# More of a fused retention and two-layer kernel's second layer by two levels of Strassen

## The chip, the cores and the metric

One core of a Trainium2 chip runs the kernel. The time is device microseconds, median of three runs. One further execution was taken by the hardware profiler; its lines are what the text reads. Engines: PE is TensorE (PEld its weight loads), DVE is VectorE, ACT ScalarE, POOL GpSimd, SP SyncE, which issues most DMAs.

## The reference

```python
# attention: B, H, S, D = 4, 8, 768, 64, one state per head with decay gamma
for t in range(S):
    state = gamma[None, :, None, None] * state + np.einsum('bhd,bhe->bhde', k[:, :, t], v[:, :, t])
    y[:, :, t] = scale * np.einsum('bhd,bhde->bhe', q[:, :, t], state)
# two layers on 3072 tokens of 512: w_in is 512 x 2048, w_out is 2048 x 512
h = x @ w_in
g = np.maximum(0.01 * h, h)
return (g @ w_out).astype(np.float32)
```

All matrix products are float32.

## The kernel before

**Chunks and units.** The sequence of 768 is cut into NC = 6 chunks of C = 128 tokens; with 4 batches a chunk is 512 tokens. The 2048 hidden columns are cut into NU = 4 units of 512. Chunks 0 and 1 are done first, together. For chunks 2 to 5 a loop over `n` from 0 to 15 runs unit `u = n % 4` of chunk `c = 2 + n // 4`; "unit 7" in this document is `n = 7`. Each unit has a first-layer part and a second-layer part, and the loop is skewed: in iteration n the second layer of unit n and the first layer of unit n + 1 are done.

**Strassen.** A 512 x 512 product of blocks of 256 is done as seven products M1 to M7 instead of eight; blocks are summed first (S and T blocks) and the seven results are summed after. In a *one-level* product each of the seven is four matmuls of 128x128 weights and 256 columns. In a *two-level* product it is again split by Strassen into seven of 128x128 weights and 128 columns. The first layer is two-level: `inner(n, 0)` does four of its seven products side by side ("group 0", 4 x 7 matmuls), `inner(n, 1)` the other three ("group 1"). Before, second-layer units 4 to 14 do M1, M5, M6 and M7 one-level (`trunk`) and M2, M3 and M4 two-level (`leaf_steps`); units 0 to 3 and 15 do all seven one-level (`output`). The profile records each float32 matmul twice, so a one-level product is 8 records and a two-level product 14.

**One iteration.** The order is written by hand, and every engine runs its own instructions in that order. In units 4 to 14: VectorE's `differences` for unit n's second layer (four), group 0 of unit n + 1 and its three VectorE sums, `outer(n + 1, 0)` (two VectorE sums); in units 0, 1, 4, 5, 8 and 9 (`visiting`) the visit of the attention for two batches of the next chunk (`joint_visit`); in `u == 1`, `differences` of the next chunk's x; in `u == 2` and `u == 3` the sums of its blocks (`sums_of_x`). Then `leaf_sums` on GpSimd (four differences, 384 columns each), three steps of the trunk, in units 0, 1, 4, 5 and 8 `scores_of_pair` for the next two batches, the rest of the trunk's sums into `o`, group 1 of unit n + 1 with three VectorE sums, `outer(n + 1, 1)` (five VectorE sums; four leaky activations on ScalarE), and the leaf: 7 x 3 matmuls.

**Banks.** Groups 0 and 1 accumulate in PSUM banks 0 to 3; in each, ScalarE copies M1's result from bank 0 into bank 3, on which M6 accumulates. M5 and M3 use bank 1, M4 bank 2. The trunk uses banks 5 (A: M1), 4 (B) and 7 (C: M5). The leaf uses 6, 7, 2 and 5. The visit uses 0, 7, 1 and 2, the scores 0 to 3. A bank is used again when its readers are done.

**The output tile.** `o` collects a chunk's result over four units; all chunks from the second on share one buffer, so the first write of a chunk (in unit 4, 8 or 12, a ScalarE copy) waits until the stores of the chunk before have left it. Leaf results go into `o` by a DMA of GpSimd that adds to its destination (`accum_op`, line 1283), except at the end of a chunk (units 7 and 11), where VectorE adds them and SyncE stores (1287, 1288).

**The attention in the loop.** `joint_visit(c, b)` ends by loading v of the pair that follows (`of_pair`, line 138, on SyncE; the buffer is free when the visit's matmuls are done) and scaling it on GpSimd (`decay_v`, 163, two instructions). `scores_of_pair` of the same iteration reads it on TensorE (382), one half for each instruction; its products of q and k come just before (371).

**Second-layer weights of the leaf.** The row sums of the weights (`sums_of_rows`, VectorE, in units 0 to 3) are written to DRAM (`leaf_kept`), and loaded before each leaf by `load_rows` (1235, SyncE): at the end of the unit before, or in the middle of a visiting unit. First-layer weights stream in as `wa` (group 0) and `wb` (group 1) by `load_unit`, also on SyncE.

**The last unit.** Unit 15 is one-level, in the order M1, M5, M6, M4, M2, M7, M3; M5 and M3 end in three pieces. Its M5 reads the first of `differences(15)`.

Of the kernel before, what the change touches and what calls it, by code (L numbers as in the profile page):

```python
# [18 lines left out]
C = 128  # L19
# [3 lines left out]
def kernel(  # L23
# [587 lines left out]
    def plus(out, a, b):  # L611
        nc.vector.tensor_tensor(out=out, in0=a, in1=b, op=ALU.add)  # L612
# [195 lines left out]
    last_three = {}  # L808
# [9 lines left out]
    def new_g(c, u):  # L818
        i = slot[0]
        slot[0] = 1 - i  # L820
        both = work.tile([128, 7, 2, N], FP32, tag=f"g{i}", name=f"g_{c}_{u}")
        last_three[c, u] = both[:, 2:5]
        return u, both[:, 0:4], Reversed(both)
# [360 lines left out]
    leaf_kept = [dram.tile([128, 3, 7, C], FP32, name=f"leaf_kept_{u}") for u in range(NU)]  # L1184
# [3 lines left out]

    def leaf_rooms():

        free = [flat_of(unit(k)[:, 2:5]) for k in (1, 3, 5)]
        spare = [x2_place[0][:, 21 * C :], streamed_flat[0][:, 21 * C :]]
        more = [spare[i // 2][:, ds(i % 2 * 3 * C, 3 * C)] for i in range(4)]
        return free, spare, [x.rearrange("p (q n) -> p q n", q=3) for x in more]

    def rows_of(u):

        if u < NU - 1:
            return [((0, 3, 1), unit(2 * u + 1)[:, 2:5])]
        return [((0, 3, 2), units[2 * u + 1][1]), ((1, 2, 1), last_s4)]  # L1200

    def sums_of_rows(u):

        free, _, more = leaf_rooms()
        if u == NU - 1:
            more = more[0:2] + [x[:, 7 * C : 10 * C].rearrange("p (q n) -> p q n", q=3)
                                for x in free[0:2]]
        bases = []
        for at, blocks in rows_of(u):
            which = slice(*at)  # L1210
            a11, a21, a12, a22 = (blocks[:, :, k, ts(m, C)] for k in range(2) for m in range(2))
            r = [x[:, which] for x in more]
            plus(r[0], a21, a22)
            minus(r[1], r[0], a11)
            minus(r[2], a12, r[1])
            minus(r[3], a11, a21)
            bases.append((which, blocks))

        def keep():
            for which, blocks in bases:  # L1220
# [4 lines left out]
            for j, r in enumerate(more):  # L1225
                nc.sync.dma_start(out=leaf_kept[u][:, :, 3 + j], in_=r)
        return keep

    def load_rows(n):

        free, spare, _ = leaf_rooms()
        leaf_weights[:] = [x[:, 0 : 7 * C].rearrange("p (j n) -> p j n", j=7)
                           for x in (free[0], free[1], spare[1])]
        for to, kept_rows in zip(leaf_weights, (leaf_kept[at_of(n)[1]][:, i] for i in range(3))):
            nc.sync.dma_start(out=to, in_=kept_rows)
# [3 lines left out]
    def by_leaves(n):  # L1239
        return n >= NU and n < N2 - 1  # L1240

    def leaf_sums(n):

        free, spare, _ = leaf_rooms()
        made = [x.rearrange("p (q n) -> p q n", q=3)
                for x in (free[0][:, 7 * C : 10 * C], free[1][:, 7 * C : 10 * C],
                          spare[0][:, 0 : 3 * C])]
        three = last_three[at_of(n)]
        b11, b12, b21, b22 = (three[:, :, k, ts(h, C)] for k in range(2) for h in range(2))
        for out, a, b in ((made[0], b12, b11), (made[1], b22, made[0]), (made[2], b21, made[1]),  # L1250
                          (b12, b22, b12)):
            nc.gpsimd.tensor_tensor(out=out, in0=a, in1=b, op=ALU.subtract)
        return [b11, b21, *made, b22, b12]

    def leaf_steps(n, moving):

        ps = [bank[i][:, 0 : 3 * C].rearrange("p (i n) -> p i n", i=3) for i in (6, 7, 2, 5)]
        results = leaf_results()
        for m, q, j, s in INNER:
            for i in range(3):  # L1260
                nc.tensor.matmul(ps[q][:, i], lhsT=leaf_weights[i][:, j], rhs=moving[s][:, i],  # L1261
# [14 lines left out]
    def leaf_results():  # L1276
        return flat_of(unit(5)[:, 2:5]).rearrange("p (i q n) -> p i q n", i=3, q=4)

    def leaf_results_taken(c, o, final):

        results = leaf_results()
        if not final:
            nc.gpsimd.dma_start(out=o[:, 0:3].rearrange("p i k n -> p (i k n)"),  # L1283
                                in_=results.rearrange("p i q n -> p (i q n)"), accum_op=ALU.add)
            return
        for i in range(3):
            plus(o[:, i], o[:, i], results[:, i].rearrange("p (k h) n -> p k (h n)", k=2))
            nc.sync.dma_start(out=out[c, i], in_=o[:, i])

    def trunk(c, o, part, first, final):  # L1290

        u, g, gd = part
        ps = {x: room[x] for x in "ABC"}
        for m, x, sa, rhs, start in (("M1", "A", 0, g[:, 0], True), ("M5", "C", 4, gd[:, 0], True),
                                     ("M6", "B", 5, gd[:, 1], False),
                                     ("M7", "B", 1, g[:, 1], False)):
# [7 lines left out]
            elif m == "M6":  # L1304
                if first:
                    nc.scalar.copy(out=o[:, 1], in_=ps["B"])
                else:
                    plus(o[:, 1], o[:, 1], ps["B"])
            elif m == "M7":
                yield  # L1310
                if first:
                    nc.scalar.copy(out=o[:, 2], in_=ps["B"])
                    plus(o[:, 3], o[:, 3], ps["B"])
                else:
                    plus(o[:, 2:4], o[:, 2:4],
                         ps["B"].unsqueeze(1).to_broadcast([128, 2, 2, N]))
                if final:
                    nc.sync.dma_start(out=out[c, 3], in_=o[:, 3])
            yield

    def trunk_taken(o, first):

        if first:
            nc.scalar.copy(out=o[:, 0], in_=room["A"])
            nc.scalar.copy(out=o[:, 3], in_=room["C"])
            plus(o[:, 1], o[:, 1], room["C"])
        else:
            plus(o[:, 0], o[:, 0], room["A"])
            plus(o[:, 1:4:2], o[:, 1:4:2],
                 room["C"].unsqueeze(1).to_broadcast([128, 2, 2, N]))  # L1330
# [43 lines left out]
    def outer(n, group, later=None):  # L1374
# [17 lines left out]
        if group == 0:  # L1392
            plus(u2, u2, m1)
            plus(to(1), u2, m5)
            return
# [47 lines left out]

    held = []
    for n in range(N2):
# [4 lines left out]
        visiting = c + 1 < NC and u < 2  # L1450
# [4 lines left out]
        if n + 1 < N2:  # L1455
# [6 lines left out]
            outer(n + 1, 0)  # L1462
        if visiting and u == 0:
            xs[c + 1] = new_x(c + 1)
        if visiting:
# [7 lines left out]
        moving = leaf_sums(n) if by_leaves(n) else None  # L1473
        scores_next = visiting and following(c + 1, 2 * u)
        part = gs.pop(n)
        if by_leaves(n):
            steps = trunk(c, os[c], part, u == 0, u == NU - 1)
# [3 lines left out]
        products(steps, 3)  # L1481
        if scores_next:
            scores_of_pair(*scores_next)
        if visiting:
            load_unit(n + 2, 0)
        if by_leaves(n):
            if scores_next and u > 0:
                products(steps, 2)
            trunk_taken(os[c], u == 0)
            if scores_next and u == 0:  # L1490
                products(steps, 2)
        else:
            products(steps, 1)
        if c == 2:
            keep = sums_of_rows(u)
        if more:
# [3 lines left out]
            if c == 2:  # L1500
                keep()
            products(steps, 1)
            later = [] if by_leaves(n) else None
            outer(n + 1, 1, later)
        if by_leaves(n):
            products(steps, 1)
# [104 lines left out]
```

## Time and profile before

| | us |
|---|---|
| median of 3 runs | 633.54 (633.47 to 634.14) |
| profiled execution | 633.81 |
| its span | 632.1 |
| TensorE busy | 624.7 |
| VectorE busy | 498.1 |
| ScalarE busy | 283.5 |
| GpSimd busy | 81.4 |

Units 0 to 15 take the span from about 251 us on. Unit 7 starts at 427.79, unit 8 at 450.33, unit 9 at 477.32, unit 12 at 548.1 and unit 15 at 616.1. A table of busy time by stretch (start:end, length, busy TensorE, weight loads, VectorE, ScalarE and GpSimd with counts, granted clock, DMA share, GB/s), of units 6, 7, 8, 9 and 12:

```profile
405.20:427.80 22.60, 22.60 (x175) 21.77 (x174) 18.93 (x33) 10.60 (x23) 5.17 (x5) 1.00 0.98 306
427.80:450.30 22.50, 22.50 (x174) 21.67 (x174) 20.55 (x28) 10.06 (x21) 5.84 (x5) 1.00 0.81 240
450.30:477.30 27.00, 27.00 (x399) 25.64 (x398) 18.24 (x33) 11.86 (x24) 6.15 (x8) 1.00 0.64 218
477.30:503.00 25.70, 25.00 (x303) 23.64 (x302) 21.35 (x33) 10.51 (x23) 5.65 (x7) 1.00 0.77 224
548.10:571.00 22.90, 22.82 (x175) 21.81 (x174) 15.91 (x26) 12.02 (x26) 5.15 (x4) 1.00 0.77 247
```

The clock column is 1.00 in all of them. In a timeline a line such as `x4` is a run of neighbouring instructions; what stands in brackets is the idle time before it and what ended it. A DMA's line on SPq or POOL is its issue; it lands later.

### The profile page before, as it was taken

Reading aid. Unit: us, or ns where it says so; the run is one execution under the profiler, and the core shown is the slowest. Engines: PE = TensorE matmul, PEld = TensorE weight load, DVE = VectorE, ACT = ScalarE, POOL = GpSimd, SP = SyncE. Lnnn points to the kernel's source line nnn. Section 1 sums busy time; section 2 is a strip of 40 time slices with the busy share of each in tenths; the row PEclk is TensorE's granted clock in tenths of the full one; section 3 lists DMA queues with packets and bytes.
Section 4 is the critical chain, followed back from the end, with each engine's and each line's share of the span. In section 5 each row is a group of like instructions: output and inputs, shape, how many; then the busy total and the mean of one; then the engine's idle time right before and its main releaser. Section 6 shows DMA issues by size and latency. Waiting matters only on the chain.

```text
span 632.1 us, 15063 instructions
## 1 busy us (share of the span) xinstructions
PE 624.7 (99%) x6284; PEld 570.5 (90%) x6284; DVE 498.1 (79%) x803; ACT 283.5 (45%) x559; POOL 81.4 (13%) x98
## 2 busy tenths in 40 slices
PE   8999999999999999999999999999999999999997
PEld 5888888888888889899999999999998999999996
DVE  5679769889979976668887768799848889866765
ACT  5876646347443114352442452634434424544540
POOL 2000000000011010101000033313033023033200
PEclk9999999999999999999999999999999999999999
DMA  8941325547772998295964888998479579689724
GB/s 330 404 138 34 133 67 208 163 145 226 260 276 81 334 350 289 89 347 168 340 209 157 280 293 250 342 293 260 157 240 306 159 230 278 206 263 271 192 45 116
DMA packets 103219, 141.18 MB, mean 223 GB/s; under 512 B 4328, under 2 KB 82024, under 8 KB 103152
## 3 DMA queue, kind: packets, MB, share of 16 engines
q1 hardware_dynamic: 101552, 132.53, 63.3%
q0 software_dynamic: 1296, 7.08, 5.6%
q8 instruction: 49, 0.80, 0.5%
q10 hardware_dynamic: 304, 0.62, 0.3%
q14 instruction: 18, 0.15, 0.1%
HBM read 108.49 MB, written 24.64 MB: 211 GB/s over the span
## 4 chain that ended last, share of the span: by engine, by line
PE 90%; DMA 5%; ACT 2%; DVE 2%; issue 0%; SPq 0%; DVEq 0%; ACTq 0%
PE bank L1348 26%; PE bank L1299 12%; PE bank L668 11%; PE bank L1261 8%; PE C_h L668 4%; PE B_o L668 4%; PE A_h L668 4%; PE A_o L668 4%; PE C_o L668 4%; PE B_h L668 4%; PE D_o L668 2%; PE D_h L668 2%; DMA x_words<-in_weights_dram 1%; DMA wa<-kept 1%; DMA in<-in_kv_dram 1%; PE bank L371 1%
## 5 line engine op out<-in xcount | busy, mean ns | idle before, releaser
L612 DVE TENSOR_TENSOR made<-made,bank 128x512 f32<-128x512 f32 (+1 forms) x96 | 56.1, 617 | 39.9 <-PE bank L1348 35.9
L1348 PEld LDWEIGHTS bank<-x,wb 128*128 128x128 f32 x672 | 77.6, 192 | 1.1 <-ACT bank L1352 0.3
L1348 PE MATMUL bank<-x,wb 128*128 128x128 f32 x672 | 77.9, 275 | 0.1
L612 DVE TENSOR_TENSOR o<-o,bank 128x512 f32<-128x512 f32 (+3 forms) x75 | 55.2, 767 | 24.3 <-ACT bank L782 6.2
L615 DVE TENSOR_TENSOR g<-g 128x512 f32<-128x512 f32 x96 | 64.1, 688 | 5.3 <-ACT g L1390 0.6
L1348 PE MATMUL bank<-x,wa 128*128 128x128 f32 x512 | 67.6, 275 | 0.0
L1299 PE MATMUL bank<-g,w 128*128 128x256 f32 x288 | 66.1, 382 | 0.7 <-DVE x L468 0.7
L1348 PEld LDWEIGHTS bank<-x,wa 128*128 128x128 f32 x512 | 62.8, 192 | 0.3
L1299 PEld LDWEIGHTS bank<-g,w 128*128 128x128 f32 x288 | 53.2, 190 | 8.0 <-DVE x L468 1.1
L1348 PE MATMUL bank<-t,wa 128*128 128x128 f32 x384 | 53.4, 275 | 0.1
L1348 PEld LDWEIGHTS bank<-t,wa 128*128 128x128 f32 x384 | 48.0, 192 | 0.3 <-DMA wa<-kept 0.3
L612 DVE TENSOR_TENSOR g<-made 128x512 f32<-128x512 f32 x64 | 44.0, 709 | 3.0
L1352 ACT COPY bank<-bank 128x512 f32<-128x512 f32 (+1 forms) x32 | 16.6, 520 | 60.1 <-PE bank L1348 59.8
L1390 ACT ACTIVATE g<-g 128x512 f32<-128x512 f32 x64 | 38.5, 631 | 8.2 <-DVE g L612 8.2
L668 PE MATMUL bank<-g,w 128*128 128x256 f32 x168 | 38.0, 382 | 0.0
L668 PEld LDWEIGHTS bank<-g,w 128*128 128x128 f32 x168 | 31.3, 190 | 4.2
L668 PE MATMUL bank<-g,last 128*128 128x256 f32 (+1 forms) x148 | 32.6, 375 | 0.0
L668 PEld LDWEIGHTS bank<-g,last 128*128 128x128 f32 x148 | 27.0, 190 | 3.9 <-DVE g L615 0.4
L1261 PE MATMUL bank<-g,w 128*128 128x128 f32 x176 | 26.8, 275 | 0.0
L668 PE MATMUL A_h<-x,w 128*128 128x256 f32 x112 | 26.6, 380 | 0.0
L1303 ACT COPY bank<-bank 128x512 f32<-128x512 f32 x11 | 6.3, 570 | 41.1 <-PE bank L1299 41.1
L1283 POOL DMA_DIRECT2D o<-w x9 | 8.1, 903 | 125.2 <-DVE g L615 65.6
(255 smaller groups left out, 1234.8 us busy)
## 6 DMA issues: line engine op xcount, KB each, us to landing
wa<-kept SPq DMA_DIRECT2D x16, 1344.0 KB, 9.4
raw<-in_weights_dram SPq DMA_DIRECT2D x31, 512.0 KB, 4.4
wb<-kept SPq DMA_DIRECT2D x16, 896.0 KB, 5.5
w<-leaf_kept SPq DMA_DIRECT2D x22, 448.0 KB, 4.6
wa<-kept SPq DMA_DIRECT2D x16, 448.0 KB, 6.1
wb<-kept SPq DMA_DIRECT2D x16, 448.0 KB, 6.3
o<-w POOLq DMA_DIRECT2D x9, 768.0 KB, 9.2
out_dram<-o SPq DMA_DIRECT2D x23, 256.0 KB, 2.5
```

The lines of the kernel that those rows point to most:

```text
L371: nc.tensor.matmul(at[j][ts(h, 64), n, m, i], lhsT=x[ts(j, 64), 1, a, ts(h, 64)], rhs=x[ts(j, 64), 0, a, ts(h, 64)], start=(n == 0 and a = ...
L612: nc.vector.tensor_tensor(out=out, in0=a, in1=b, op=ALU.add)
L615: nc.vector.tensor_tensor(out=out, in0=a, in1=b, op=ALU.subtract)
L668: nc.tensor.matmul(to, lhsT=block(w, sa)[:, k, ts(i, 128)], rhs=rhs[:, k, a:z], start=(first and (i == 0 or split) and n == 0 and k == 0), ...
L1261: nc.tensor.matmul(ps[q][:, i], lhsT=leaf_weights[i][:, j], rhs=moving[s][:, i], start=(i == 0 and m in ("M1", "M5", "M4")), stop=True, sk ...
L1283: nc.gpsimd.dma_start(out=o[:, 0:3].rearrange("p i k n -> p (i k n)"), in_=results.rearrange("p i q n -> p (i q n)"), accum_op=ALU.add)
L1299: nc.tensor.matmul(ps[x][:, i, :], lhsT=block(2 * u + 1, sa)[:, k, ts(i, 128)], rhs=rhs[:, k, :], start=(start and i == 0 and k == 0), sto ...
L1303: nc.scalar.copy(out=ps["B"], in_=ps["A"])
L1348: nc.tensor.matmul(ps[q][:, i], lhsT=w[:, j, i], rhs=part_of(moving[i], s), start=(i == 0 and m in ("M1", "M5", "M4")), stop=True, skip_gr ...
L1352: nc.scalar.copy(out=ps[3], in_=ps[0])
L1390: nc.scalar.activation(g[:, i], g[:, i], AF.Prelu, alpha=0.01)
```

## The change

Units 2 to 14 are now done by leaves (`ON_CHIP`, `by_leaves`), and M7 joins M2, M3 and M4 in the leaf, which is 7 x 4 matmuls over 512 columns; the trunk keeps M1, M5 and M6. All four results go through `results` (512 columns wide), whose third block gets the fourth added by VectorE, and always by the accumulating DMA into all of `o`; at the end of a chunk, now also in unit 3, four stores on SyncE follow that DMA. The sums of the trunk go into `o` after its third step: in the first unit of a chunk by two ScalarE copies (512 and 1536 wide) and one VectorE sum, else by VectorE sums of 512, 1024 and 1536. The scores come after two trunk products instead of three.

Rows of M7 are summed and kept as well (four blocks; the sets for units 0 and 1 of a chunk with block M7 apart, in room left by the tile `u2`). The sets for u = 2 and 3 stay in one place in unit 1's weight tile for the leaves of units 2 and 3; set 1 and set 2 are both made in unit 1, set 3 on GpSimd in unit 3 (12 instructions). In unit 9 the first of GpSimd's differences waits for the last VectorE sum of `outer(n + 1, 0)`.

```diff
-        last_three[c, u] = both[:, 2:5]
+        last_four[c, u] = both[:, 1:5]
...
+    ON_CHIP = range(2, NU)
+    def by_leaves(n):
+        return ON_CHIP[0] <= n < N2 - 1
...
-    def sums_of_rows(u):
+    def sums_of_rows(u, engine=nc.vector):
...
+        if u in ON_CHIP:
+            flat = free[1].rearrange("p (r q n) -> p r q n", r=4, q=4)
+            parts = [(slice(0, 4), [flat[:, r] for r in range(4)])]
+        else:
+            (_, blocks), = rows
+            rows = [(slice(0, 1), blocks[:, 0:1]), (slice(1, 4), blocks[:, 1:4])]
...
+            for n, a, b in ((0, a21, a22), (1, r[0], a11), (2, a12, r[1]), (3, a11, a21)):
+                engine.tensor_tensor(out=r[n], in0=a, in1=b, op=ALU.subtract if n else ALU.add)
...
+            for which, r in parts:
+                for j in range(4):
+                    nc.sync.dma_start(out=leaf_kept[u][:, which, 3 + j], in_=r[j])
...
-    def leaf_sums(n):
+    def leaf_sums(n, behind=None):
...
-            nc.gpsimd.tensor_tensor(out=out, in0=a, in1=b, op=ALU.subtract)
+            op = nc.gpsimd.tensor_tensor(out=out, in0=a, in1=b, op=ALU.subtract)
+            if behind is not None:
+                tc.add_manual_dep(op.ins, behind.ins.name, IN_ORDER, reason="one port for both")
+                behind = None
...
+    TARGETS = (3, 0, 1, 2)
...
-            for i in range(3):
-                nc.tensor.matmul(ps[q][:, i], lhsT=leaf_weights[i][:, j], rhs=moving[s][:, i],
+            for i, to in enumerate(TARGETS):
+                nc.tensor.matmul(ps[q][:, to], lhsT=leaf_weights[i][j], rhs=moving[s][:, i],
...
-    def leaf_results_taken(c, o, final):
-
-        results = leaf_results()
-        if not final:
-            nc.gpsimd.dma_start(out=o[:, 0:3].rearrange("p i k n -> p (i k n)"),
-                                in_=results.rearrange("p i q n -> p (i q n)"), accum_op=ALU.add)
-            return
-        for i in range(3):
-            plus(o[:, i], o[:, i], results[:, i].rearrange("p (k h) n -> p k (h n)", k=2))
-            nc.sync.dma_start(out=out[c, i], in_=o[:, i])
+    def leaf_results_taken(n, o):
+
+        c, u = at_of(n)
+        results = leaf_results(n)
+        plus(results[:, 2], results[:, 2], results[:, 3])
+        nc.gpsimd.dma_start(out=o.rearrange("p i k n -> p (i k n)"),
+                            in_=results.rearrange("p i q n -> p (i q n)"), accum_op=ALU.add)
+        if u == NU - 1:
+            for i in range(4):
+                nc.sync.dma_start(out=out[c, i], in_=o[:, i])
...
     def trunk_taken(o, first):
+        def to(part, n):
+            return room[part].unsqueeze(1).to_broadcast([128, n, 2, N])
         if first:
             nc.scalar.copy(out=o[:, 0], in_=room["A"])
-            nc.scalar.copy(out=o[:, 3], in_=room["C"])
-            plus(o[:, 1], o[:, 1], room["C"])
+            nc.scalar.copy(out=o[:, 1:4], in_=to("B", 3))
         else:
             plus(o[:, 0], o[:, 0], room["A"])
-            plus(o[:, 1:4:2], o[:, 1:4:2],
-                 room["C"].unsqueeze(1).to_broadcast([128, 2, 2, N]))
+        plus(o[:, 1:4:2], o[:, 1:4:2], to("C", 2))
+        if not first:
+            plus(o[:, 1:4], o[:, 1:4], to("B", 3))
...
-            outer(n + 1, 0)
+            outer_done = outer(n + 1, 0)
...
         if by_leaves(n):
-            steps = trunk(c, os[c], part, u == 0, u == NU - 1)
+            moving = leaf_sums(n, outer_done if visiting and not scores_next else None)
+            steps = trunk(*part)
...
-        products(steps, 3)
+        products(steps, 2 if by_leaves(n) else 3)
         if scores_next:
             scores_of_pair(*scores_next)
         if visiting:
             load_unit(n + 2, 0)
+        products(steps, 1)
         if by_leaves(n):
-            if scores_next and u > 0:
-                products(steps, 2)
             trunk_taken(os[c], u == 0)
...
-        if c == 2:
-            keep = sums_of_rows(u)
+        keep = {0: lambda: [sums_of_rows(0)], 1: lambda: [sums_of_rows(1), sums_of_rows(2)],
+                3: lambda: [sums_of_rows(3, nc.gpsimd)]}.get(n, list)()
...
-            for count, ready in ((4, 3), (1, 1)) if scores_next else ((1, 1), (3, 2), (1, 1)):
+            for count, ready in ((4, 3), (1, 1)):
...
-            leaf_results_taken(c, os[c], u == NU - 1)
-        if more and by_leaves(n + 1) and not (at_of(n + 1)[0] + 1 < NC and at_of(n + 1)[1] < 2):
+            leaf_results_taken(n, os[c])
+        if by_leaves(n + 1) and n + 1 >= NU and not visits(n + 1):
             load_rows(n + 1)
```

The weights of the leaf of units 2 and 3 are read where they stand; from unit 4 on they are loaded as before, in four pieces of 448 KB instead of three.

## The prediction

> **What bounds the kernel now.** I read the page first: busy shares, then clock and DMA by slice.
>
> ```profile
> span 632.1 us, 15063 instructions
> PE 624.7 (99%) x6284; PEld 570.5 (90%) x6284; DVE 498.1 (79%) x803; ACT 283.5 (45%) x559; POOL 81.4 (13%) x98
> PEclk9999999999999999999999999999999999999999
> o<-w POOLq DMA_DIRECT2D x9, 768.0 KB, 9.2
> ```
>
> TensorE is busy 99% at the full granted clock, so only less TensorE work, or a wait put into it, moves the time. Next, the chain of waits in units 7 and 8 (start us, us, what). A unit starts with the first product of group 0 for the next unit; t is time from there.
>
> ```profile
> 427.79 6.25 PE bank L1348 x56
> 434.04 5.18 PE bank L1299 x24
> 439.22 4.69 PE bank L1348 x42
> 443.91 1.73 PE bank L1299 x8
> 445.64 4.69 PE bank L1261 x42
> 450.33 6.25 PE bank L1348 x56
> 464.00 1.09 PE bank L371 x64
> 465.09 0.93 PE bank L382 x32
> ```
>
> Nothing lies between the pieces. A one-level product is 8 records, 1.727 us (5.18/3). A two-level product is 14 records of 128 columns: 6.25/56 = 0.1116 each, 1.562 us; the three-wide form gives the same (4.69/42). Then I read the timeline for what is hidden: SyncE's issues, GpSimd and VectorE (start, us, engine, line).
>
> ```profile
> 431.56 1.36 DVE L615 TENSOR_TENSOR x<-x 128x384 f32<-128x384 f32 x1
> 436.65 1.87 DVE L612 TENSOR_TENSOR made<-made,bank 128x512 f32<-128x512 f32 x3
> 452.21 1.54 SPq L1288 DMA_DIRECT2D out_dram<-o  x3
> 458.73 0.34 SPq L138 DMA_DIRECT2D v<-in_kv_dram  x1
> 462.46 2.04 POOL L163 TENSOR_TENSOR v<-v,dec 128x512 f32<-128x512 f32 x2 [4.52 <-DMA v<-in_kv_dram]
> 464.91 1.11 PE L382 MATMUL bank<-v,k 64*64 64x64 f32 x32
> 617.79 0.88 POOL L1283 DMA_DIRECT2D o<-w  x1 [16.42 <-DVE g L615]
> 623.69 2.04 DVE L612 TENSOR_TENSOR o<-o,bank 128x512 f32<-128x512 f32 x3 [3.03 <-DMA o<-w]
> ```
>
> In unit 8 v is loaded, decayed on GpSimd (done 463.5 and 464.5) and read by TensorE at 464.9 (second half 465.4): cover about 1 us. At the end the accumulating transfer takes 5.9 us with the queues empty, and VectorE waits 3.03 us for it.
>
> **The change, part by part.**
>
> *TensorE.* Units 4 to 14 turn one product each, units 2 and 3 four each: 19 x (1.727 - 1.562) = **3.14 us** less. Unit 9 now takes 25.73 us; unit 7's 22.54 plus a visit (2.04: the chain's pieces from 456.58 to 458.62 in unit 8) and one switch to the trunk's product (1.92 where 1.73 is usual, 0.2) is 24.77, so **0.96 us** of stall goes if GpSimd starts behind the outer sums (VectorE's two there took 1.43 and 1.30 beside GpSimd, 0.69 alone). Unit 12 holds 0.34 us above its neighbours. Gain at most **4.44 us**.
>
> *Stores of a finished chunk.* This decides. Now VectorE adds the last leaf results and SyncE stores at t 1.9 of units 8 and 12 (452.21 - 450.33). In the new code a GpSimd accumulating transfer comes between, and four stores stand in SyncE's in-order queue waiting for it, also after unit 3. VectorE: three sums 128 wider (+0.3) and one more (0.65), so the transfer is issued at t 1.7 + 0.95 = 2.65, with VectorE's lateness below 3.3. It grows from 768 to 1024 KB: 5.8 us (nothing added) to 5.8 x 4/3 = 7.7 with empty queues, 9.2 x 4/3 = 12.3 at the median's traffic. SyncE has nothing else in flight then, so I take 6.7. Landed 10.0; four issues of 0.4: 11.7.
>  Queued behind: unit 8's v. Issued 11.7 instead of 8.4, 3.7 to land (458.73 to 462.46), 1.0 and 2.04 of decay: second half ready 17.5. The change also moves the scores one product (1.73) earlier, so TensorE wants it at 465.4 - 450.3 - 1.7 = 13.5. **Unit 8: 4.0 us** (2.5 to 5.4, more with traffic). In unit 4 VectorE is later (worked below: last result at 3.7, issue 4.3): landed 11.0, stores out 12.7, v 16.4, second decay 18.45. The visit itself waits 0.6 for VectorE to leave bank 1 (group-0 sums there from 6.6 to 8.5), so v is wanted at 14.1: 4.4 + 0.6, **unit 4: 5.0** (3 to 6.5). Unit 5 stores nothing, but its decays run beside VectorE's differences of x (390.18 to 393.2) and end at t 15.0; wanted 13.5: **unit 5: 1.5** (1.0 to 1.8). Unit 9 has no scores: 0. Also behind the stores in units 4 and 8 stand four row loads and wa: rows issued by 14, landed by 21, wanted when the leaf starts at 16.0 + 4.0 + 4.7 = 24.7; wa issued by 15, landed (9.4 to 11.9) by 27, wanted at 31. Covered by the wait for v itself, and late by 3 us if that were gone.
>  Unit 12 has no visit. ScalarE's first copy into o waits for the stores, and behind it on ScalarE stand group 1's five copies out of PSUM, without which TensorE's banks don't come free: last issued 11.3, landing 2.2: 13.5. Copies of 512 (0.59) and 1536 (from 0.48 at 384 and 0.59 at 512: 1.44) end at 15.5, then the M1 copy of group 1 at 16.1; its M6 wants that at 11.43 + 2.01 = 13.44. **Unit 12: 2.7** (1 to 4.5). Its leaf rows follow the stores on SyncE: 11.7 + 1.2 + about 6 = 19, against a leaf start at 16.1 + 2.7 = 18.8: nothing added.
>  Last unit: the transfer, issued 2.8, lands 9.5 (now 7.6), and all of VectorE's sums into o now wait for it, the three pieces of M5 (0.81) too; VectorE reaches the last three at 13.5 where it now ends at 12.7. Also the extra sum delays differences(15): the first is done at t 2.9, M5 wants it at 1.73. **End: 1.5** (0.7 to 2.5), the larger covering the other.
>
> *VectorE and GpSimd.* A unit's trunk and leaf sums are 5.45 us now (0.68, 1.21, 0.68, 1.21, three of 0.55); 0.68 + 1.21 + 1.75 (1536 wide, from 0.68 and 1.21) + three of 0.65 + 0.65 = 6.2 after. GpSimd's four differences go from 384 to 512 elements: 1.00 each to between 1.04 (L163, 512 wide) and 1.33 (proportion); I take 1.3, being the nearest operation. They now also need the last of VectorE's differences. Two SBUF operands on VectorE make it alternate: in unit 7 the four x sums took 431.56 to 436.65, 1.27 a pair where 0.55 is normal; 1.57 with wider GpSimd ops. Rows of PSUM sums do not stretch (1.87 for three beside GpSimd).
>  Units 6 to 7 by queue: result 2.2, differences to 5.0, group-0 sums to 7.6, two outer sums beside GpSimd to 10.3, x sums behind its last to 14.6, trunk sums 18.2, group-1 sums 19.8, outer 23.1, leaf sums and result 25.7, which is t 3.3 of unit 7 (22.37 after). There: differences 6.2, x sums 11.5 to 12.4, group-0 sums 13.4 to 14.3; group 1's M5 wants bank 1 at 12.1 and M6 bank 3 (plus a copy) at 13.4. **Units 7 and 11: 1.0 each** (0 to 1.5).
>  Unit 1 gets two sets of row sums: 1.1 + 2.2 + 2.8 = 6.1 for 2.2 now, 1.2 of it in idle time. The last leaky of unit 1 ends 308.3 instead of 306.8, and the copy queued behind it on ScalarE 308.9 against 307.83 wanted: **unit 2: 1.25** with 0.2 for bank 7 (0 to 2). VectorE is then at t 3.9 in unit 3, where group-0 sums end about 14.5 (1.6) and GpSimd's twelve row differences (0.45 and 0.78 by proportion) make the leaf wait 0.6: **unit 3: 2.2** (0 to 4). SyncE's 16 row stores in unit 1 (6 now, +2.24 MB at 350 GB/s, 6.4 us) push wa from 310.8 to about 317; landing 9.4: 326.4, wanted 328.9; nothing, 3 us if it slips.
>
> [...]
>
> Sum: 4.0 + 5.0 + 1.5 + 2.7 + 1.5 + 2 x 1.0 + 1.25 + 2.2 = 20.15 of new waits, less 4.44: **+15.7 us** on the profiled 632.1 span (633.81 with what lies around it, 0.27 above the median). 633.54 + 15.7 = 649.2; I say **649**.
>
> **Rivals.**
> - *Only the stores' chain costs.* For: VectorE is busy 18.9 of 22.6 us in unit 6 and 20.6 of 22.5 in unit 7 (busy time by stretch), idle time which may take what I charge. Against: the idle time lies behind the x sums, where TensorE is not waiting. Units 4 and 8 then cost 3.5 each (transfer issued 2.8), 5 1.5, 12 2.2, end 1.5: 12.2 - 4.4 = +7.8: 641.3.
> - *SyncE's queue holds nothing up* (other side). If the transfer lands within 3.9 us of issue (t 6.7), v is issued at 8.4 as now. Units 4 and 8 keep 0.6 each, unit 5 1.0, 12 0.2, end 0.7: 3.1; with VectorE's terms at their low bound, 0: -1.3: 632.2. For: output stores land in 2.5. Against: no o transfer landed under 5.8.
> - *Traffic.* The transfer lands in 12.3: units 4, 8 and 12 each 5.6 worse: 666. For: the median of 9.2; against: those run beside row loads, which now stand behind it.
> - *The change saves no TensorE time*: four-wide groups might cost more than 0.1116 a record; group 0 is four-wide and does not.
>
> **How the numbers follow.** Forecast 0.64, first rival 0.18, second 0.12, third 0.06. The forecast's own range is 643 to 656; the first rival takes it to 640. Range 640 to 656. A difference within 0.2% (1.3 us) is what a measurement cannot tell from none. The second rival's 632.2 sits at that edge: faster 0.09, same 0.04; slower 0.87.
>
> **What would show it.** SyncE's v issue in units 4 and 8 right behind four stores at t 11 to 13, and TensorE waiting at L382 for GpSimd; ScalarE idle before the first copy into o of unit 12, on a DMA; group 1 waiting for VectorE in units 3, 7 and 11; unit 9 about 24.6 long; units 6, 10 and 13 at 22.4. Wrong if v's issue in unit 8 stays near t 8.4, or the accumulating transfer lands in under 5 us.

## The result, and the profile after

The changed kernel takes 666.29 us (median of 4 runs, 660.31 to 666.66) beside 633.50 for the kernel before on the same chip: 1.0493 times as long, 95% interval 1.0434 to 1.0553. The profiled execution is the 660.31 one, span 658.6. The other three have mean granted clocks of 0.979 to 0.982 where it has 0.988; at half clock or full, that is 24 to 28 us at half clock in place of 16. If TensorE had work all that time, it lost 4 to 6 us by it, about what these runs are longer; this is an estimate, since no profile shows where it fell.

The page after, the same lines as before:

```profile
span 658.6 us, 15393 instructions
PE 629.7 (96%) x6398; PEld 576.6 (88%) x6398; DVE 522.7 (79%) x799; ACT 293.5 (45%) x561; POOL 115.7 (18%) x122
PEclk9999999999999999999999799999999999989999
o<-w POOLq DMA_DIRECT2D x13, 1024.0 KB, 8.9
```

TensorE was idle for 7 us of the span before and is for 29 now; and the clock, full in every slice before, falls in two. The waits of TensorE by line and releaser (us in total, times, longest):

```profile
PE bank L382 <- POOL v L163: 9.7, 6, 6.1
PE bank L1359 <- ACT bank L1363: 3.8, 2, 3.5
PE bank L1322 <- issue: 3.5, 1, 3.5
PE bank L1289 <- DVE o L612: 1.3, 1, 1.3
...
PE bank L668 <- DVE o L612: 1.1, 1, 1.1
PE bank L668 <- DVE g L615: 1.1, 1, 1.1
PE bank L1289 <- POOL w L1233: 0.6, 1, 0.6
```

The first is the scores' wait for v, 6.1 us in unit 4, 1.5 and 1.8 in units 5 and 8; the second is unit 12's; the third, ahead of the trunk of unit 8, has no semaphore behind it; the two at L668 are the last unit's; L1289 is the leaf of units 2 and 3. How the chain in unit 8 runs (timeline: start, us, engine, line; units start at 353.46, 462.57 and 566.96 for 4, 8 and 12):

```profile
465.52 0.90 POOL L1309 DMA_DIRECT2D o<-w  x1 [13.56 <-DVE w L612]
...
474.26 1.80 SPq L1313 DMA_DIRECT2D out_dram<-o  x4
...
474.38 5.41 PE L1322 MATMUL bank<-g,w 128*128 128x256 f32 x16 [3.53 <-issue]
...
476.17 0.72 SPq L138 DMA_DIRECT2D v<-in_kv_dram  x1
...
481.23 2.04 POOL L163 TENSOR_TENSOR v<-v,dec 128x512 f32<-128x512 f32 x2 [11.06 <-DMA v<-in_kv_dram]
...
482.32 0.68 PE L382 MATMUL bank<-v,k 64*64 64x64 f32 x16 [1.45 <-POOL v L163]
...
581.50 0.58 ACT L1335 COPY o<-bank 128x512 f32<-128x512 f32 x1 [5.95 <-DMA out_dram<-o]
581.99 1.45 ACT L1336 COPY o<-bank 128x1536 f32<-128x1536 f32 x1
583.32 0.50 ACT L1363 COPY bank<-bank 128x384 f32<-128x384 f32 x1
...
583.87 4.58 PE L1359 MATMUL bank<-x,wb 128*128 128x128 f32 x24 [3.46 <-ACT bank L1363]
```

The transfer is issued at 465.52, the stores that wait for it at 474.26 (8.7 us on), v right behind them, and v's second half is decayed at 483.27: 20.7 us into the unit. The largest wait of TensorE in unit 8 is not the one for v: 3.53 us pass ahead of the trunk first. But v comes last all the same, and TensorE waits 1.8 us more for it (1.45 and 0.32), so v's arrival sets the length of this unit, whatever stood ahead of it. In unit 12 ScalarE's copy into `o` waits for the stores, the M1 copy of group 1 stands behind it, and TensorE waits 3.46 us for that one. The table by stretch, in the form shown of before (span, busy engines, then granted clock, DMA share, GB/s):

```profile
353.50:389.00 35.50, 29.18 (x436) 27.29 (x435) 18.59 (x30) 12.46 (x23) 8.12 (x9) 0.90 0.91 276
...
440.20:462.60 22.40, 22.40 (x180) 21.78 (x180) 21.64 (x30) 11.00 (x22) 6.78 (x5) 1.00 0.96 273
462.60:497.10 34.50, 29.20 (x404) 27.05 (x403) 18.33 (x30) 12.86 (x24) 8.12 (x9) 0.95 0.74 225
497.10:522.20 25.10, 24.90 (x308) 23.95 (x308) 23.52 (x32) 10.74 (x22) 7.29 (x7) 1.00 0.85 245
567.00:594.70 27.70, 24.24 (x180) 23.43 (x179) 16.14 (x23) 12.76 (x24) 6.69 (x5) 0.94 0.83 251
```

These are units 4, 7, 8, 9 and 12. Unit 7 is the 22.4 that the saved product gives; units 4, 8 and 12 hold 21 of the 26.5 us that the span is longer, and in them the clock is under 1. Cut to where it fell:

```profile
370.20:377.00 6.80, 3.93 (x69) 3.46 (x70) 1.38 (x2) 0.00 (x0) 4.86 (x5) 0.52 0.84 295
475.60:479.20 3.60, 3.60 (x11) 2.86 (x10) 0.00 (x0) 0.57 (x1) 0.00 (x0) 0.53 1.04 342
584.90:588.30 3.40, 3.40 (x19) 3.40 (x18) 0.55 (x1) 0.95 (x2) 0.00 (x0) 0.50 1.08 362
```

Each stands behind (or over the end of) an idle stretch of TensorE of 6.08, 3.53 and 3.46 us; behind the second, the 16 records of trunk from 474.38 on take 5.41 us where 16 take 3.45 at full clock (5.18 for 24). The half clock lasts 6.83, 3.41 and 3.41 us, and again from 656.56 to the end, where TensorE has no work left (its last matmul ends at 654.2). What it costs is less than half of these times: in unit 4 TensorE still waits for v until 373.07, and in unit 8 the half clock ends at 479.06, ahead of the wait for v that begins at 480.87, so there the wait takes it up.

Lengths of units in the traces (from the start of group 0 to the next such start; "end" is units 14 and 15). The runs of the experiments are named as below:

| unit | before | after | e1_direct | e2_late | e5_scores3 | e8_no_behind | e10_from3 | e12_fill_all |
|---|---|---|---|---|---|---|---|---|
| 2 | 23.03 | 24.53 | 24.27 | 24.54 | 24.40 | 24.54 | 23.03 | 24.41 |
| 3 | 23.03 | 23.69 | 23.70 | 23.69 | 23.69 | 23.69 | 23.60 | 23.70 |
| 4 | 26.98 | 35.57 | 29.47 | 43.13 | 33.13 | 28.77 | 28.11 | 34.34 |
| 5 | 27.06 | 28.78 | 28.78 | 30.44 | 27.05 | 27.05 | 27.05 | 28.66 |
| 7, 11 | 22.54 | 22.38 | 22.38 | 22.38 | 22.4 | 22.38 | 22.4 | 22.4 |
| 8 | 27.00 | 34.52 | 29.82 | 40.55 | 35.99 | 28.93 | 27.37 | 33.10 |
| 9 | 25.73 | 25.12 | 25.31 | 24.71 | 24.60 | 26.16 | 26.46 | 24.60 |
| 12 | 22.88 | 27.73 | 22.60 | 36.02 | 27.86 | 22.60 | 22.60 | 26.68 |
| end | 38.73 | 41.69 | 41.25 | 41.71 | 41.70 | 39.03 | 39.08 | 45.63 |

### The profile page after: what moved, and what is told of

It reads as the page before. It is cut to its first block, busy times and chain, and to the rows that moved or that the text cites. A ratio compares the mean times of both kernels' runs of the same rounds, so it can differ in the third digit from the quotient of the medians.

```text
span 658.6 us, 15393 instructions
## 1 busy us (share of the span) xinstructions
PE 629.7 (96%) x6398; PEld 576.6 (88%) x6398; DVE 522.7 (79%) x799; ACT 293.5 (45%) x561; POOL 115.7 (18%) x122
## 4 chain that ended last, share of the span: by engine, by line
PE 75%; DMA 10%; DVE 6%; issue 4%; ACT 2%; POOL 2%; SPq 1%; DVEq 0%; POOLq 0%; ACTq 0%
PE bank L1359 21%; PE bank L1289 11%; PE bank L1322 8%; PE C_h L668 4%; PE B_o L668 4%; PE A_h L668 4%; PE A_o L668 4%; PE C_o L668 4%; PE B_h L668 4%; PE bank L668 3%; DMA o<-w 3%; DMA v<-in_kv_dram 2%; PE D_o L668 2%; PE D_h L668 2%; DMA x_words<-in_weights_dram 1%
## 5 line engine op out<-in xcount | busy, mean ns | idle before, releaser
L1359 PE MATMUL bank<-x,wb 128*128 128x128 f32 x672 | 80.3, 279 | 3.6 <-ACT bank L1363 3.5
L612 DVE TENSOR_TENSOR o<-o,bank 128x512 f32<-128x512 f32 (+4 forms) x58 | 53.4, 950 | 28.0 <-ACT o L1336 11.7
L1322 PE MATMUL bank<-g,w 128*128 128x256 f32 x240 | 57.1, 394 | 3.5 <-issue 3.5
L1322 PEld LDWEIGHTS bank<-g,w 128*128 128x128 f32 x240 | 46.3, 197 | 10.3 <-issue 3.7
L612 DVE TENSOR_TENSOR g<-made 128x512 f32<-128x512 f32 x64 | 47.3, 760 | 3.7 <-ACT bank L1293 0.5
L1289 PE MATMUL bank<-g,w 128*128 128x128 f32 x400 | 48.8, 275 | 0.0
L1289 PEld LDWEIGHTS bank<-g,w 128*128 128x128 f32 x400 | 46.8, 192 | 0.0
L1309 POOL DMA_DIRECT2D o<-w x13 | 11.7, 899 | 168.4 <-DVE w L612 168.4
L1300 ACT COPY w<-bank 128x512 f32<-128x512 f32 x52 | 30.3, 582 | 15.2 <-PE bank L1289 15.2
L612 DVE TENSOR_TENSOR w<-w,bank 128x512 f32<-128x512 f32 x39 | 25.1, 683 | 5.7 <-PE bank L1289 4.7
L163 POOL TENSOR_TENSOR in<-in,dec 128x512 f32<-128x512 f32 x2 | 2.2, 1136 | 139.9 <-DMA raw<-in_weights_dram 139.9
L668 PE MATMUL A_h<-x,w 128*128 128x256 f32 x112 | 26.6, 380 | 0.0
```

The source lines that it names most:

```text
L163: engine.tensor_tensor(out=v, in0=v, in1=gk[c].unsqueeze(2).to_broadcast([128, H, D]), op=ALU.mult)
L612: return nc.vector.tensor_tensor(out=out, in0=a, in1=b, op=ALU.add)
L668: nc.tensor.matmul(to, lhsT=block(w, sa)[:, k, ts(i, 128)], rhs=rhs[:, k, a:z], start=(first and (i == 0 or split) and n == 0 and k == 0), ...
L1289: nc.tensor.matmul(ps[q][:, to], lhsT=leaf_weights[i][j], rhs=moving[s][:, i], start=(i == 0 and m in ("M1", "M5", "M4")), stop=True, skip ...
L1300: nc.scalar.copy(out=results[:, :, {"M5": 3, "M4": 2, "M6": 1, "M2": 0}[m]], in_=ps[q])
L1309: nc.gpsimd.dma_start(out=o.rearrange("p i k n -> p (i k n)"), in_=results.rearrange("p i q n -> p (i q n)"), accum_op=ALU.add)
```

## The experiments

**Is it the stores' chain? e1_direct.** In `leaf_results_taken`:

```diff
+        if u == NU - 1:
+            for i in range(4):
+                plus(o[:, i], o[:, i], results[:, i].rearrange("p (k h) n -> p k (h n)", k=2))
+                nc.sync.dma_start(out=out[c, i], in_=o[:, i])
+            return
         nc.gpsimd.dma_start(out=o.rearrange("p i k n -> p (i k n)"),
                             in_=results.rearrange("p i q n -> p (i q n)"), accum_op=ALU.add)
-        if u == NU - 1:
-            for i in range(4):
-                nc.sync.dma_start(out=out[c, i], in_=o[:, i])
```

> Only the end of a chunk is as before the change: after units 3, 7 and 11 VectorE adds the four result blocks into o and SyncE stores each at once, with no accumulating transfer between. All the rest is the changed kernel. Theory (the stores that wait for the accumulating transfer hold up SyncE's queue and the o buffer, and the clock falls only behind the stalls that this makes): units 4, 8 and 12 lose 8.2, 7.1 and 4.8 us against the changed kernel (35.6, 34.5 and 27.7 long there), the granted clock stays at 1.00 in all three, and the time is about 640. Rival (VectorE being later and the scores coming one product earlier make the waits of units 4 and 8): these two stay over 30 us and the time is above 647.

Measured: 645.09 us (644.07 to 646.98), 1.0191 of before (1.0173 to 1.0209), clock 1.00 throughout, unit 12 at 22.60. The chain is worth 21 us of the median's 33. But units 4 and 8 stop at 29.5 and 29.8, 2 us above what was expected: the theory holds for unit 12 and the clock, the rival has a part of the other two. The waits of TensorE show which:

```profile
PE bank L429 <- DVE made L612: 3.1, 3, 1.7
PE bank L382 <- POOL v L163: 2.3, 5, 1.2
```

VectorE, with five sums of results where it had three, comes late to the group-0 sums whose banks the visit uses.

**The same part alone in the kernel before: e4_before_accum.** There the three blocks go into `o` by the accumulating transfer, and three stores follow it.

> The kernel before with one part of the change alone: after units 7 and 11 the leaf's results (three blocks, 768 KB) go into o by the accumulating transfer and three stores follow it on SyncE. Theory (the stores behind the transfer are the main cost): unit 8 waits 2 to 3 us for v, unit 12 some 2 us for ScalarE's copy into o, no stall reaches 3.4 us, so the clock stays at 1.00, and the time is 637 to 640. Rival (this part costs little without the rest of the change): the time is within 1.3 us of 633.5.

Measured: 634.86 us, 1.0021 (1.0011 to 1.0031); unit 8 is 0.88 longer, all else as before. The rival was right, and the timeline shows why the same construction costs 8 us in the one kernel and 1 in the other (unit 8 starts at 450.08):

```profile
451.80 0.90 POOL L1286 DMA_DIRECT2D o<-w  x1 [15.73 <-DVE g L615]
...
457.57 2.35 SPq L1289 DMA_DIRECT2D out_dram<-o  x3
460.02 0.39 SPq L138 DMA_DIRECT2D v<-in_kv_dram  x1
...
463.87 2.04 POOL L163 TENSOR_TENSOR v<-v,dec 128x512 f32<-128x512 f32 x2 [6.20 <-PE bank L1300]
```

The 768 KB transfer takes 5.8 us from issue to the stores, against 8.7 for 1024 KB; v is there after at most 3.85 us (GpSimd then starts on it), against 5.1; the transfer goes out 1.2 us earlier in the unit; and the scores come a product later. Second half of v ready: 15.8 us into the unit, 20.7 in the changed kernel.

**Out of the queue's way: e2_late.** The stores of a chunk are put off to behind v, the row loads and wa of the next unit:

```diff
+        while stores_left:
+            last_c, last_o = stores_left.pop()
+            for i in range(4):
+                nc.sync.dma_start(out=out[last_c, i], in_=last_o[:, i])
         products(steps, 1)
         if by_leaves(n):
             trunk_taken(os[c], u == 0)
```

> The accumulating transfer stays, but the four stores of chunks 2 and 3 are issued by SyncE in units 4 and 8 only behind v, the row loads and wa; unit 12 is as in the changed kernel. If the queue alone is at fault: v is issued at about 8.4 us into units 4 and 8, TensorE's wait for v falls from 6.1 to under 1.0 in unit 4, both units are about 27.5 to 28 long, unit 12 keeps its wait, and the time is about 646. If the o buffer is just as much at fault: ScalarE's first copy into o comes late instead, group 1 waits for it by 2 us or more in units 4 and 8, and the time is above 650.

Measured: 683.88 us, 1.0791 (1.0769 to 1.0813), the slowest of all. TensorE's wait for v in unit 4 falls to 1.0 us as the theory says, but the rival decides, and by far more than "2 us":

```profile
371.30 3.77 SPq L1503 DMA_DIRECT2D out_dram<-o  x4
...
383.00 0.58 ACT L1336 COPY o<-bank 128x512 f32<-128x512 f32 x1 [18.94 <-DMA out_dram<-o]
```

Issued behind the loads, the stores also land behind them, about 8 us after the last of them is issued; ScalarE waits, and group 1 with it, for 12.5, 7.0 and 11.0 us in units 4, 8 and 12 (unit 12, which the expectation left as it was, has its stores put off by the edit too). One `o` means that the stores cannot be late either.

**The scores' place: e5_scores3 and e6_direct_scores3.** One line, `products(steps, 2 if by_leaves(n) else 3)` back to 3; the second run has e1's stores as well.

> The changed kernel with the scores behind three trunk products instead of two; transfer and stores as changed. Theory (TensorE's wait for v is the lateness of v against the place of the scores, and moving them 1.73 us later takes that much off each): the waits for v fall from 6.1 to about 4.3 us in unit 4, from about 5 to 3.3 in unit 8, and from 1.5 to under 0.3 in unit 5; unit 12 is unchanged; with the half clock behind the shorter stalls shorter too, the time is 649 to 656. Rival (the scores' place does not matter, since bank or queue waits take up the difference): units 4, 5 and 8 within 0.5 us of the changed kernel's and the time above 658.

> Direct stores at the end of a chunk (as in the first experiment) and the scores behind three trunk products. Theory: unit 5 loses its 1.5 us wait for v (27.2 long), units 4 and 8 lose 0.5 and 0.3 and keep 1.3 and 1.7 us of waiting at the visit's first products, for VectorE, which adds the results and then the group-0 sums; the time is 641 to 643. Rival (the scores' wait only moves to group 1's products behind them): unit 5 stays above 28.3 and the time is 644 to 646.

Measured: 656.40 us, 1.0357 (1.0334 to 1.0381), and 642.17, 1.0132 (1.0101 to 1.0163). Unit 5 is 27.05 in both: its 1.5 us of waiting goes with the scores' place alone. In e5_scores3 unit 4 waits 4.57 for v and unit 8 3.18 behind a stall of 2.88, as expected; the median is just above what the theory gave, 649 to 656; unit 8 then runs 6.83 us at half clock and is longer than in the changed kernel. The time of e6_direct_scores3 came as expected, and its waits at the visit (1.26 and 1.77 us), but in its profile unit 8 is 30.39, longer than in e1_direct: 3.41 us at half clock stand behind the wait of 1.77.

**What is left on VectorE: e7_all, e9_hybrid, e10_from3.** e7_all adds three edits to e6_direct_scores3: in units 4 and 8 `differences` behind the group-0 sums; unit 14's result added by VectorE behind `differences(15)`, no transfer; set 2's row sums on GpSimd in unit 2.

> The kernel of the run before this one, with three more parts: in units 4 and 8 VectorE's differences come behind the group-0 sums; the last unit's differences come ahead of unit 14's result, which VectorE adds into o itself, with no transfer; and the row sums of set 2 are made on GpSimd in unit 2 instead of on VectorE in unit 1. Theory (VectorE's order is what is left): the waits of 1.3 and 1.7 us in units 4 and 8 go, the two of 1.05 us in the last unit go, unit 2's 1.1 goes, and the time is 634 to 637. Rival (each of these only shifts VectorE's lateness to its next reader): at least half of the 6 us stays and the time is above 639.

Measured: 639.16 us, 1.0085 (1.0070 to 1.0100). The last unit's edit works (39.04 for 41.26). The other two only move the lateness, as the rival says: in units 4 and 8 the waits of 1.3 and 1.8 for the banks become these,

```profile
PE bank L1324 <- DVE x L468: 3.6, 2, 1.8
```

and unit 2 gets worse (26.37; its leaf waits 2.13, and 3.41 us at half clock follow) while unit 3 loses its wait (22.38).

e9_hybrid: at the end of a chunk the transfer carries blocks 0 and 1 alone, VectorE adds blocks 2 and 3, which are stored first; e10_from3 also has `ON_CHIP = range(3, NU)`, unit 2 as before.

> Scores behind three products, the last unit with unit 14's result added by VectorE, and at the end of a chunk half of each: the accumulating transfer carries only the first two result blocks (512 KB), VectorE adds the other two (three sums of 512, as many as the kernel before has there), and SyncE stores those first. Theory (the transfer's size and VectorE's count of sums set the waits of units 4 and 8): the transfer lands within 5 us, v is issued at 8.4 to 9 us into units 4 and 8, the waits of 1.3 and 1.8 us for VectorE at the visit go as well, the two units are 27.0 to 27.5 long, and the time is 635 to 637. Rival (any accumulating transfer ahead of the stores holds up v): a wait for v of over 1 us in unit 4 or 8, or over 3 us more in both units together than in the kernel before, and the time is above 638.

> The run before this one, with unit 2 done by seven one-level products again and its row sums made by VectorE in unit 2 (as in the kernel before), so the leaf starts with unit 3. Theory (the two sets of row sums in unit 1 and GpSimd beside VectorE's x sums make unit 2's and 3's waits): unit 2 is 23.0 to 23.4 long instead of 24.5, unit 3 22.4 to 23.4, and the time is 632.5 to 635, at or near the kernel before. Rival (unit 3's wait is GpSimd's own twelve row differences and stays, and the row sums in unit 2 stall unit 3 by VectorE): unit 3 above 23.6 and the time above 635.5.

Measured: 639.02 us, 1.0086 (1.0074 to 1.0098), and 636.81, 1.0043 (1.0030 to 1.0056). In both the waits for v and for VectorE in unit 4 are under 0.4 each, though unit 4 stays at 28.2 and 28.1 (v goes out 9.3 us into it in e9_hybrid); what else it spends the time on was not found. In unit 8 of e9_hybrid 1.05 us of waiting for VectorE are left. Unit 2 returns to 23.03 in e10_from3, unit 3 hardly moves (GpSimd's twelve row differences, a wait of 0.96). Neither reached its expected time: stalls of 0.95 (e9_hybrid, unit 8) and 1.70 (e10_from3, unit 9) stand in the profiles as "issue", with no semaphore behind them. By its own signs e9_hybrid goes to the rival: units 4 and 8 together are 57.3 us, 3.3 more than in the kernel before, and the time is above 638, but hardly any of it is a wait for v (0.3).

**GpSimd behind the outer sums: e8_no_behind and e11_before_behind.** The first takes the wait out of a repaired version, the second puts it alone into the kernel before (`leaf_sums(n, outer_done if n == 9 else None)`).

> Direct stores, scores behind three products, and the last unit as in the run before this one; in unit 9 GpSimd's differences do not wait for VectorE's outer sums. Read by units: unit 9 alone bears on that wait. Theory (without it VectorE's two outer sums stretch beside GpSimd and the visit waits for bank 7): a gap of 0.7 us or more ahead of unit 9's visit or trunk, unit 9 0.8 to 1.1 us longer than with the wait. Rival (the wait does nothing): unit 9 within 0.3 us of the other runs' (25.1 to 25.3). The last unit's two waits of 1.05 us should be gone here too.

> The kernel before with one part of the change alone: in unit 9 GpSimd's first difference waits for the last of VectorE's two outer sums. Theory (the two sums take 0.69 us each instead of 1.43 and 1.30, so the trunk's first product no longer waits for VectorE): the gap of 0.7 us in unit 9 goes, unit 9 is 24.8 to 25.1 long instead of 25.73, all other units are as before, and the time is 0.7 to 1.0 us lower, 632.5 to 633.0, the lowest of all. Rival (the differences, now later, hold up the leaf or push VectorE's differences of x later, and these a bank): unit 9 or 10 gives it back and the time is 633.3 or more.

Measured: e8_no_behind takes 638.95 us, 1.0090 (1.0069 to 1.0111), its last unit 39.03. Unit 9 is 26.16 without the wait, against 25.31 in e6_direct_scores3; alone in the kernel before it takes unit 9 from 25.73 to 24.76, and the time to 632.86 beside 633.61, ratio 0.9991 (0.9983 to 1.0000). VectorE's two outer sums, without the wait (e8_no_behind) and with it (e11_before_behind):

```profile
490.35 1.75 DVE L612 TENSOR_TENSOR made<-made 128x512 f32<-128x512 f32 x1
492.21 1.57 DVE L612 TENSOR_TENSOR g<-made 128x512 f32<-128x512 f32 x1
```

```profile
486.98 0.69 DVE L612 TENSOR_TENSOR made<-made 128x512 f32<-128x512 f32 x1
487.78 0.69 DVE L612 TENSOR_TENSOR g<-made 128x512 f32<-128x512 f32 x1
```

Of the two parts tried alone in the kernel before (this and e4_before_accum) it is the one that pays, and the fastest version found; its 0.97 us in the unit is clear, its gain in the whole time is at the edge of what the runs can tell.

**The clock: e3_fill and e12_fill_all.** Matmuls that nothing reads, into a free bank, ahead of the products of v and of group 1's fourth:

```diff
+        for _ in range(dummies.pop((c, b), 0)):
+            fill_bank(bank[6].rearrange("p (i n) -> p i n", n=C))
         for n in range(2):
             key, val = keys.pop((c, b + n)), vals[c, b + n]
```

> The changed kernel with matmuls that nothing reads put into two of TensorE's waits: 24 bfloat16 matmuls of 128x512 (some 0.22 us each, 5.2 us together) ahead of the products of v in unit 4, 11 (2.4 us) ahead of the fourth product of group 1 in unit 12. No wait is taken away. Theory (an idle stretch of TensorE of about 3.4 us or more is followed by stretches of 3.41 us at half clock): the half clock of 6.83 us in unit 4 and of 3.41 us in unit 12 is gone, the units are 3.4 and 1.7 us shorter, and the time falls by about 5 us. Rival (the lower clock comes from something else that these units hold, and costs what it costs either way): the clock records stay and the time is the same or longer.

> The changed kernel with matmuls that nothing reads (bfloat16, 128x512, about 0.2 us each) in three of TensorE's waits: 26 ahead of the products of v in unit 4, 22 there in unit 8, 16 ahead of the fourth product of group 1 in unit 12. Theory (half clock follows an idle TensorE; with work in the waits it stays at full clock and each wait still ends when what it waits for is there): no half clock in units 4, 8 and 12, and the time is 4 to 6 us under the changed kernel's 660.3 (its fastest): 654 to 657. Rival (the half clock comes with these units' load on the memory or with the scores' small matmuls, as it did in unit 5 and unit 8 of the other run with such matmuls): stretches of half clock stay in units 4, 5 or 8, and the time is 659 or more.

Measured: 662.52 us, 1.0451 (1.0426 to 1.0476), and 659.93, 1.0411 (1.0396 to 1.0426). The first was spoiled by what it left unfilled: units 4 and 12 have no half clock and are 1.4 and 0.7 us shorter, less than half of the 3.4 and 1.7 expected, but unit 8's wait is 6.8 us in that profile, followed by 10.24 us at half clock. The theory's 3.4 us is about the shortest idle stretch with half clock behind it in the changed kernel's trace, 3.46; other runs had it behind shorter ones too (last section). With all three filled (e12_fill_all, the same places; 26 of the added matmuls took 5.79 us and 16 took 3.62, 0.22 to 0.23 each):

```profile
372.00:380.00 8.00, 6.87 (x102) 5.82 (x101) 2.59 (x3) 2.60 (x4) 7.05 (x6) 1.00 0.91 303
479.00:486.00 7.00, 6.22 (x65) 5.21 (x63) 1.60 (x2) 2.39 (x4) 6.84 (x6) 1.00 1.06 380
575.00:590.00 15.00, 14.68 (x112) 12.29 (x110) 5.99 (x9) 7.55 (x14) 0.71 (x1) 1.00 1.03 347
```

Full clock, units 4, 8 and 12 shorter by 1.2, 1.4 and 1.0. In units 4 and 12 what TensorE waited for came no earlier than before (v's second half 20.5 us into unit 4, 20.6 in the changed kernel; the restart of group 1 17.0 us into unit 12, 16.9 there), so there the 1.2 and 1.0 are the clock. In unit 8 they are not: here v itself came earlier (unit 8 starts at 461.59, the transfer is issued at 464.54).

```profile
472.07 1.87 SPq L1316 DMA_DIRECT2D out_dram<-o  x4
...
478.82 2.04 POOL L163 TENSOR_TENSOR v<-v,dec 128x512 f32<-128x512 f32 x2 [9.64 <-DMA v<-in_kv_dram]
```

The transfer took 7.5 us where it took 8.7, and v's second half was ready 19.3 us into the unit where it was 20.7: the 1.4 us. The four runs lie within 659.5 to 660.4 where the changed kernel's spread over 6 us. The expected 654 to 657 was missed because the last unit, left unfilled, waited 3.2 us on a transfer of 9.2 us there, and had 6.83 us at half clock behind it.

## Why the prediction was right and wrong

It said 649 (+15.7) on the slower side; the profiled execution came out 26.5 longer, and the median 32.8. The main mechanism, v and ScalarE's copy held up behind the accumulating transfer and its stores, was right, and the size was half. Step by step, where "measured" is a unit's added length with the products' saving of 0.165 each put back:

| step | predicted | measured |
|---|---|---|
| a product by leaves | -0.165 | -0.16 (units 6, 7, 10, 11, 13) |
| unit 9's stall goes | -0.96 | -0.97 alone (e11_before_behind), about half of it here |
| unit 2, unit 3 | 1.25, 2.2 | 2.2, 1.3 |
| units 7 and 11 | 1.0 each | 0 |
| unit 4 | 5.0 | 8.8, of it 1.2 by the clock |
| unit 5 | 1.5 | 1.9 |
| unit 8 | 4.0 | 7.7, none of it shown to be the clock |
| unit 12 | 2.7 | 5.4 with the 0.34 that was to go, 1.0 by the clock |
| end | 1.5 | 3.1, of it two waits of 1.05 |

- **The step that failed by its size: "SyncE has nothing else in flight then, so I take 6.7".** With quiet queues the transfer took 7.1 us (unit 12) and 7.0 (last unit, issue to VectorE's first sum), above the 6.7 taken, if below the 7.7 of proportion; in units 4 and 8 it took 8.8 and 8.7. In unit 4 SyncE did have something in flight: the four stores of unit 3's row sums, issued from 351.67 to 356.35. In unit 8 the queues were quiet, but a 16 KB load of instructions ran from 471.99 to 472.88, and the transfer's last 8 KB packet from 472.86 to 473.72, when all its others of that size had ended at 472.16; without that tail an estimate from these times is 7.2 us, as in unit 12. And "3.7 to land" for v, from a queue with nothing ahead of it, became 5.3 and 5.1 behind four stores and beside the row loads. Together v's second half was ready at 20.6 and 20.7 us into the units, where 18.45 and 17.5 were worked out: 2.1 and 3.2 us of the 3.8 and 3.7 that these units were short. e4_before_accum carries this: with 768 KB and v there in 3.85, the same order of waits costs 0.9.
- **The step that was missing: every stall was priced at its own length.** Half clock behind the stalls adds 1.2 us in unit 4 and 1.0 in unit 12 by e12_fill_all, 2.2 of the 26.5; in unit 8 the wait for v takes it up, and at the end there is no matmul left under it. The runs of 666 have more half clock, at a cost that no profile shows. The profile of before shows 1.00 everywhere, and its longest wait of TensorE in the units is 0.7 us (unit 9, `PE bank L1299 <- DVE x L468: 0.7, 1, 0.7`); nothing there could price it. The trace of the changed kernel shows the half (0.50 to 0.53 in the three stretches cut out above) and steps of 3.41 us.
- **The last unit.** Its two waits of 1.05 us (VectorE's late differences, then the transfer) were to cover one another; in the trace they add up, and 0.7 us more pass behind VectorE's last sum than in the kernel before.
- **Units 7 and 11.** VectorE's x sums beside GpSimd took about 1.5 us a pair, as predicted (1.57), and the group-0 sums ended at 12.4 into unit 7, not 13.4 to 14.3, since the differences ended at 5.5 and not 6.2; the bank was wanted at 12.1 and its own sum, the first of three, was done by then. The low bound (0) was the right value. That sums out of PSUM do not stretch beside GpSimd holds in unit 12 of the kernel before, where three of 128x512 took 1.88 us (from 553.83) beside GpSimd's differences; the three of 1.87 at 436.65, quoted for it, began when GpSimd had ended (436.31).
- **Units 2 and 3** add up to the 3.45 predicted; the split was wrong. Unit 2's leaf waited for VectorE's trunk sums (1.31) as well as for ScalarE (0.34).
- **The rivals.** "Only the stores' chain costs" had the right places (its 1.5 for unit 5 too) and the same small sizes. "Traffic", 666, matched the median by accident: the transfers measured here took 7.0 to 9.2 us and not 12.3, and the median holds half clock that this rival does not have. That GpSimd's 512-wide difference would take 1.3 was right (1.26 to 1.28).

## What to carry to other kernels

A transfer that moves into a chain must be priced at its new size, with what stands ahead of it in the queues at that moment, and so must the load behind it: in units 4 and 8 the two landings were taken 1.4 to 2.1 us too short each, which made v 2.1 and 3.2 us later than forecast. A stall put into a TensorE that was never idle can cost more than its length (here 1.2 and 1.0 us more, behind stalls of 6.08 and 3.46), unless a later wait takes that up. And one output buffer bounds a store from both sides: too early holds up the queue, too late holds up the next writer.

## What the runs showed of the hardware

- **Idle and clock.** In the unit loop of these kernels all eleven idle stretches of 3.18 us and more (6.08, 3.53 and 3.46 in the changed kernel; 12.5, 11.0 and 7.0 in e2_late; 6.8 in e3_fill; 4.57, 3.7 and 3.18 in e5_scores3; 3.2 in e12_fill_all) were followed by half clock, in stretches of 3.41, 6.83, 10.24 or 13.65 us. Of those between 1.70 and 2.88 us some were (1.77 in e6_direct_scores3, 2.13 in e7_all) and some were not (1.70 in e10_from3, 1.8 in unit 12 of e3_fill, 2.88 in e5_scores3); what sets these apart no run here settles. In unit 5 of e2_late and e3_fill half clock came with idle of only 1.2 and 0.3 us around the scores' 64x64 matmuls.
- **The accumulating transfer** moves 1024 KB at some 0.2 MB/us in the trace of the changed kernel's unit 12 (packets from 571.39 to 576.57), with nothing beside it, where loads in the same unit move 0.35 to 0.4.
- **Stalls without a semaphore** of 0.95 to 3.53 us stood ahead of trunk products in four kernels (3.53 in the changed kernel, the 3.5 "issue" above; 2.88 in e5_scores3, 1.70 in e10_from3, 0.95 in e9_hybrid). In all four a 16 KB load of instructions had landed 1.36 to 1.50 us before TensorE went on (in the changed kernel at 472.88, TensorE at 474.38), which fits a wait for instructions but does not show it; that the load came late behind the transfer was not tested either.
